# A recurrent attention block with a mixture of depths: weight loads on other turns, one product piece and one pair of PSUM banks exchanged

## The chip, the cores and the metric

The kernel runs on one core of a Trainium2 chip. The metric is the device time of one execution in microseconds, given as the median of several runs. Chunks, turns and batches are counted from 0.

## What is computed

For 4 batches, 8 heads and 768 time steps, with heads of 48, a recurrence carries a state matrix along the sequence:

```python
for t in range(S):
    cur = np.einsum('bhd,bhe->bhde', u[None] * kt, vt)
    y[:, :, t] = np.einsum('bhd,bhde->bhe', rt, state + cur)
    state = wt[:, :, :, None] * state + np.einsum('bhd,bhe->bhde', kt, vt)
```

The heads side by side make rows x of 384. In each batch the 128 rows with the highest score go through a two-layer network (384 to 1024 to 384), all others are left as they are:

```python
scores = np.einsum('bsd,d->bs', x, w_gate)
h = np.maximum(xe @ w1, 0.0)
ye = h @ w2
out[b, top_idx] = x[b, top_idx] + g[:, None] * ye   # g: sigmoid of the score
```

All data are float32.

## The kernel before

The sequence is cut into chunks of 128 steps: 6 to a batch, 24 in all (`N`). A chunk is computed with matrix products, and the state passes from chunk to chunk.

**The turn.** `turn(i)` (L661) writes out by hand the order in which instructions of several chunks are issued; each engine then works through its own list in that order. It runs for i from -2 to 24. Of what a turn holds, these steps matter here:

- `scores(i)` (L337) makes `ps_s`; `masked(i)` (L347) multiplies it on VectorE into `sc`.
- `compared(i - 2)` (L462) transposes the scores of a chunk's rows into `ps_e` (L478, TensorE), counts on VectorE which rows beat which (L480, L484), and keeps a copy by ScalarE (L489). In turn 23 there is a second one, for chunk 22, after `outputs_t(23)` (L695).
- `rows_out(i - 1)` (L390) transposes a chunk's results into `ps_y`, adds a part on GpSimd, or on VectorE in the last two turns (L401), and stores the rows (L408). In those two turns `row_scores_soon` (L425) makes the rows' scores on VectorE as well.
- `inputs_t` (L307) transposes r of chunk i + 1, and at the end of the turn k of chunk i + 2, into `ps_t`. `decays_t` (L245) does the same with the decays, and `scans` (L249) makes their running products on VectorE, both for chunk i + 2. `own_products` (L315, GpSimd) multiplies r and k of chunk i + 1.
- `outputs_t(i)` (L364) makes `ps_yt` from `sc`, v and the state; `carry_products(i)` (L445) makes `ps_kv`, though not for a batch's last chunk.
- `loads(i + 5)` (L140) issues four transfers of 192 KB from SyncE: v of chunk i + 3, k and r of chunk i + 4, w of chunk i + 5. k, r and w have four buffers each, v five.
- `load_weights(1)` (L711) issues, from turn 2 on, one of seven pieces of the two weight matrices in each turn, also from SyncE: three of w1 with 512 KB and then four of w2 with 384 KB.

SyncE issues all loads, weight pieces and stores in one order. Two more kinds of DMA, the gather of the picked rows and the scatter of their results, are issued by GpSimd.

**The mixture.** When a batch's last chunk has been compared, `mixture(b)` (L491) ranks its rows (`ps_r`, `rank`), finds the indices of the picked ones (`ps_i`, `idx`), gathers them (`xe`, L546) and transposes them (`ps_x`, then `xeT`, L557). `forward` (L578) then is a Python generator of pieces. Eight pieces of first-layer products (L590) come first, each of six matmuls into a quarter of a tile `ps_h`. The first four pieces fill one tile and the last four another, and after each tile ScalarE takes the ReLU into `hid` (L595). Eight pieces of second-layer products (L600) into `ps_f` follow. VectorE then makes `ye` (L607) from `ps_f`, and GpSimd scatters it (L610). `fed(n)` (L638) issues the next n pieces, and `fed_in_turn` (L653) does so twice in a turn. For batch 2 some pieces are kept for the end: of its first-layer pieces the fourth and fifth come in turn 23, the sixth and seventh in turn 24, and the last one after the loop, with the second layer.

**The banks.** All eight PSUM banks are taken. Tiles with the tag "m" share the one bank of `psM`, and tiles with the tag "y" that of `psY`. A tile's first matmul waits until the tile before it in that bank has been read. `ps_h` and `ps_f` are tiles of `psM`, `ps_y` of `psY`. `ended` is filled after the last turn (L719), when `ps_y` isn't needed any more; from then on a second tile of `ps_h` is made in `psY`. Batch 3, the last one, goes through `forward` wholly after that.

Of the kernel before, what the change touches and what calls it, by code (L numbers as in the profile page):

```python
# [38 lines left out]
def kernel(  # L39
# [47 lines left out]
    NCH = S // L  # L87
    HP = H // 2
    NDC = C // L
    NFC = F // L  # L90
# [13 lines left out]
    psY = ctx.enter_context(tc.tile_pool(name="psY", bufs=1, space=PSUM))  # L104
    psK = ctx.enter_context(tc.tile_pool(name="psK", bufs=1, space=PSUM))
    psM = ctx.enter_context(tc.tile_pool(name="psM", bufs=1, space=PSUM))

    chunks = [(b, ci) for b in range(B) for ci in range(NCH)]
    N = len(chunks)
# [30 lines left out]
    def loads(n):  # L140
        load(v_bufs, v, n - 2)
        load(k_bufs, k, n - 1)
        load(r_bufs, r, n - 1)
        load(w_bufs, w, n)
# [12 lines left out]
    for bufs, x, n in ((r_bufs, r, 1), (w_bufs, w, 2), (v_bufs, v, 0)):  # L157
# [8 lines left out]
    weights = [  # L166
        (w1[:, i, :], moe_w1[i * L:(i + 1) * L, :]) for i in range(NDC)
    ] + [
        (w2[:, i:i + 2, :], moe_w2[i * L:(i + 2) * L, :].rearrange("(n p) c -> p n c", p=L))
        for i in range(0, NFC, 2)  # L170
    ]

    def load_weights(n):
        while n > 0 and weights:
            to, src = weights.pop(0)
            nc.sync.dma_start(out=to, in_=src)
            n -= 1
# [54 lines left out]
    def warm(n):  # L232

        ps = psM.tile([L, 512], FP32, tag="m", name="ps_n")
        for _ in range(n):
            nc.tensor.matmul(ps, nothing[:, 0:L], nothing, start=True, stop=True)
# [39 lines left out]
    def check_sums():  # L276

        above = setup.tile([L, 1], FP32)
        nc.vector.tensor_reduce(out=above, in_=guard, axis=AX.X, op=ALU.add)
        below = setup.tile([L, 1], FP32)  # L280
        junk = setup.tile([L, N * HP], FP32)
        nc.vector.tensor_scalar(
            out=junk, in0=alls.rearrange("p n j -> p (n j)"), scalar1=float(LOW ** L),
            scalar2=None, op0=ALU.is_lt, op1=ALU.add, accum_out=below,
        )
        return above, below
# [291 lines left out]
    def forward(b, n, idx, xe, xeT, gate, gated):  # L578

        hid = mod.tile([L, NFC, L], FP32, name="hid")
        for f0 in range(0, NFC, 4):

            pool, tag = (psY, "y") if ended and f0 % 8 == 4 else (psM, "m")
            ps = pool.tile([L, 4, L], FP32, tag=tag, name="ps_h")
            for q in range(4):
                for dc in range(NDC):
                    nc.tensor.matmul(  # L590
                        ps[:, q, :], w1[:, dc, (f0 + q) * L:(f0 + q + 1) * L],
                        xeT[:, dc, :], start=(dc == 0), stop=(dc == NDC - 1),
                    )
                if q == 3:
                    nc.scalar.activation(out=hid[:, f0:f0 + 4, :], in_=ps, func=AF.Relu)  # L595
                yield q == 3

        ps = psM.tile([L, C], FP32, tag="m", name="ps_f")
        for fc in range(NFC):
            nc.tensor.matmul(  # L600
                ps, hid[:, fc, :], w2[:, fc, :], start=(fc == 0), stop=(fc == NFC - 1)
            )
            yield fc == NFC - 1
        while not gated:
            mix()
        ye = mod.tile([L, C], FP32, name="ye", bufs=2)
        nc.vector.scalar_tensor_tensor(  # L607
            out=ye, in0=ps, scalar=gate, in1=xe, op0=ALU.mult, op1=ALU.add
        )
        nc.gpsimd.indirect_dma_start(  # L610
            out=views[b][0:b + 1].rearrange("b s c -> (b s) c"),
            out_offset=bass.IndirectOffsetOnAxis(ap=idx[0:n, 0:1], axis=0),
            in_=ye[0:n], in_offset=None,
            bounds_check=(b + 1) * S - 1, oob_is_err=False,
        )
        yield True
# [3 lines left out]
    mixing, picked, feed, ended, sums = [], [], [], [], []  # L620

    def step(f, n, *more):
        if 0 <= n < N:
            f(work.setdefault(n, dict(n=n)), *more)

    def mix(n=1, place=None):


        while n > 0 and mixing:
            if place is not None and mixing[0][1] not in (None, place):  # L630
                return
            try:
                mixing[0][1] = next(mixing[0][0])
                n -= 1
            except StopIteration:
                mixing.pop(0)

    def fed(n, on=True):  # L638

        while n > 0:  # L640
            if not feed:
                if not picked:
                    return
                feed.append((picked[0][0], forward(*picked.pop(0))))
            try:
                last = next(feed[0][1])
                n -= 1
                if last and not on:
                    return
            except StopIteration:  # L650
                feed.pop(0)

    def fed_in_turn(n, few):  # L653

        kept = (feed or picked) and (feed or picked)[0][0] == B - 2
        fed(few if kept else n, on=False)

    PIECES = -(-2 * NFC * len(groups) // NCH)


    def turn(i):  # L661
        soon = i >= N - 1
        step(first_left, i + 1)
        step(own_products, i + 1)
        step(scores, i)
        step(own_values, i)
        step(carry, i - 1, work.get(i))
        step(scaled, i + 1, "K", "right")
        step(own_weights, i + 1)
        if soon:  # L670
            step(masked, i)
        if i == N - 1:
            sums.extend(check_sums())
        if i < N:
            step(compared, i - 2)
        if not soon:
            step(masked, i)
        step(back, i)
        if i == 0:
            warm(6)  # L680
        mix(place="half")
        step(rows_out, i - 1, soon)
        step(row_scores_soon if soon else row_products, i - 1)
        step(own_results, i)
        fed_in_turn(PIECES // 2, 2 if i >= N - 1 else 1)
        step(inputs_t, i + 1, "R", r_bufs)
        if i == -1:
            warm(4)
        step(scaled, i + 1, "R", "left")
        step(decays_t, i + 2)  # L690
        mix(place="mid")
        if i == -2:
            warm(2)
        step(range_check, i + 2)
        step(outputs_t, i)  # L695
        if i == N - 1:
            step(compared, i - 1)
        step(carry_products, i)
        fed_in_turn(PIECES - PIECES // 2, 1 if i == N - 1 else 0)
        step(inputs_t, i + 2, "K", k_bufs)  # L700
        if i == -2:
            warm(1)
        if not soon:
            step(row_sums, i - 1)
        step(scans, i + 2)
        if 0 <= i - 2 < N - 1 and chunks[i - 2][1] == NCH - 1:
            mixing.append([mixture(chunks[i - 2][0]), "end"])
        mix(place="end")
        if i > -2:
            loads(i + 5)  # L710
        if i > 1:  # L711
            load_weights(1 if NCH > 2 else 100)

    with tc.manual_schedule():
        warm(6)
        for i in range(-2, N + 1):
            turn(i)

        ended.append(True)  # L719
        mix(1000)  # L720
        mixing.append([mixture(B - 1), "half"])
        step(compared, N - 1)
        fed(1)
        mix()
        wide = checked(sums)
        fed(1)
        mix()
        fed(NFC - 2)
        mix(2)
        fed(2)  # L730
        mix(1000)
        fed(1000)
        outside = nc.values_load(wide, min_val=0, max_val=1)
# [72 lines left out]
```

## Time and profile before

| what | value |
|---|---|
| median of 3 runs | 207.44 us (207.41 to 207.98) |
| the profiled execution | 208.35 us |
| its span, first to last instruction | 206.6 us |
| mean granted TensorE clock | 0.994 |
| busy: PE / DVE / ACT / POOL | 193.0 / 161.4 / 123.4 / 133.2 us |
| DMA moved | 29.20 MB in 105,671 packets, 100,512 of them under 512 B |
| share of the hardware queue q1 | 71.4% of 16 engines' span |
| weight pieces, issue to landing | 5.9 us (512 KB), 5.0 us (384 KB) |
| loads of k, issue to landing | 5.2 us |

PE is TensorE's matmuls, PEld its weight loads, DVE VectorE, ACT ScalarE, POOL GpSimd, SP SyncE; SPq is SyncE issuing DMAs. Times in the views are microseconds from the span's start. In a list in order of time each line gives start, length, engine, line of the kernel and operation, then what is written and read; in square brackets stands how long the engine idled before it and what ended that. Matmuls are pipelined, so two neighbours overlap by a tenth or two. The row of DMA shares cuts the span into 40 slices of 5.2 us; a digit is the busy share of the DMA engines in tenths.

Turns can be told apart by their `ps_s`: that of turn 0 starts at 9.54 us, of turn 5 at 40.25, of turn 7 at 52.31, of turn 10 at 75.99, of turn 23 at 173.18. The first first-layer product of batch 0 starts at 73.95, its first second-layer product at 95.54.

### The profile page before, as it was taken

What the parts mean: (1) busy time and instruction counts of PE and PEld (TensorE: products, weight loads), DVE (VectorE), ACT (ScalarE), POOL (GpSimd) and SP (SyncE); (2) the same over time, 40 slices, a digit from 0 to 9 for tenths busy, and PEclk for the clock granted to TensorE, in tenths of its full rate; (3) what the DMA queues carried; (4) which work ended last, traced back from release to release, by engine and by line L of the source; (5) the groups of instructions that cost most, each with busy time, mean ns of one, the idle gap of its engine ahead of it and who ended that gap; (6) DMA issues with size and microseconds to landing.
All of it is one profiled execution on the core that took longest, in us unless ns stands there. A gap on an engine that the chain in (4) does not pass through costs nothing.

```text
span 206.6 us, 6425 instructions
## 1 busy us (share of the span) xinstructions
PE 193.0 (93%) x2302; PEld 157.1 (76%) x2303; DVE 161.4 (78%) x350; ACT 123.4 (60%) x642; POOL 133.2 (64%) x165
## 2 busy tenths in 40 slices
PE   7999999988889899999999999999999999898980
PEld 3668888767777788898887888897787898775940
DVE  5999999999979968988869888979868984851010
ACT  7177977768754765878355866787545776310300
POOL 6366899886847996668538898668638896122101
PEclk9999999999999999999999999999999999999997
DMA  6999999798988999998992994998553211111101
GB/s 113 186 163 177 167 179 203 187 168 233 248 188 182 241 237 193 202 193 180 208 155 77 154 203 99 132 179 150 121 86 90 56 49 41 38 43 40 38 8 43
DMA packets 105671, 29.20 MB, mean 141 GB/s; under 512 B 100512, under 2 KB 104864, under 8 KB 105632
## 3 DMA queue, kind: packets, MB, share of 16 engines
q1 hardware_dynamic: 105120, 27.14, 71.4%
q0 software_dynamic: 512, 1.57, 2.5%
q8 instruction: 20, 0.33, 0.7%
q14 instruction: 19, 0.16, 0.3%
HBM read 23.20 MB, written 5.51 MB: 139 GB/s over the span
## 4 chain that ended last, share of the span: by engine, by line
PE 77%; DMA 9%; SPq 4%; DVE 2%; POOL 2%; issue 2%; ACT 1%; POOLq 0%; DVEq 0%
PE ps_t L242 12%; PE ps_h L590 11%; PE ps_f L600 11%; PE ps_s L342 11%; PE ps_yt L375 10%; DMA k_buf<-in_k_dram 9%; PE ps_yt L383 5%; PE ps_y L242 5%; PE ps_w L242 4%; PE ps_kv L437 4%; SPq L135 3%; PE ps_e L478 3%; PE ps_r L504 1%; ACT rk L327 1%; PE ps_x L555 1%
## 5 line engine op out<-in xcount | busy, mean ns | idle before, releaser
L327 ACT ACTIVATE rk<-rk 128x48 f32<-128x48 f32 x192 | 43.6, 231 | 0.0
L327 ACT ACTIVATION_READ_ACCUMULATOR rk<-rk 128x1 f32 x192 | 36.3, 189 | 0.0
L407 POOL TENSOR_TENSOR x<-x,vo 128x384 f32<-128x384 f32 x22 | 22.1, 1005 | 21.0 <-ACT x L405 20.8
L266 DVE TENSOR_TENSOR_SCAN left<-ps_w,from_left 128x511 f32<-128x511 f32 x24 | 30.7, 1281 | 0.9
L388 ACT COPY yt<-ps_yt 128x512 f32<-128x512 f32 x24 | 14.0, 585 | 28.3 <-PE ps_yt L383 25.0
L255 DVE TENSOR_TENSOR_SCAN right_buf<-ps_w,from_right 128x511 f32<-128x511 f32 x24 | 29.1, 1212 | 1.7 <-PE ps_w L242 1.7
L318 POOL TENSOR_TENSOR rk<-r_buf,k_buf 128x384 f32<-128x384 f32 x24 | 24.2, 1007 | 9.1 <-DMA r_buf<-in_r_dram 9.1
L350 DVE TENSOR_TENSOR sc<-ps_s,before_f 128x1024 f32<-128x1024 f32 x24 | 29.3, 1220 | 0.8 <-PE ps_s L342 0.8
L342 PE MATMUL ps_s<-R,K 48*128 48x128 f32 x384 | 27.9, 285 | 0.3 <-ACT yt L388 0.2
L375 PE MATMUL ps_yt<-sc,v_buf 128*64 128x128 f32 x384 | 26.3, 278 | 1.4 <-PE ps_w L242 1.2
L342 PEld LDWEIGHTS ps_s<-R,K 48*128 48x128 f32 x384 | 23.3, 187 | 3.9 <-issue 2.5
L590 PE MATMUL ps_h<-xeT,w 128*128 128x128 f32 x192 | 25.3, 279 | 0.8 <-DVE ye L607 0.8
L321 POOL TENSOR_TENSOR rk<-rk,u_bc 128x384 f32<-128x384 f32 x24 | 24.1, 1004 | 2.4 <-DMA u_bc<-in_u_dram 1.8
L375 PEld LDWEIGHTS ps_yt<-sc,v_buf 128*64 128x64 f32 x384 | 20.6, 136 | 5.7 <-issue 2.7
L590 PEld LDWEIGHTS ps_h<-xeT,w 128*128 128x128 f32 x192 | 23.0, 192 | 2.0 <-ACT xeT L557 1.4
L600 PE MATMUL ps_f<-w,hid 128*128 128x384 f32 x64 | 23.8, 499 | 0.0
L412 POOL TENSOR_TENSOR scr<-x,wg_bc 128x384 f32<-128x384 f32 x22 | 22.0, 1002 | 1.7
L333 POOL TENSOR_TENSOR vo<-v_buf,own 128x384 f32<-128x384 f32 x24 | 20.0, 832 | 1.6 <-ACT rk L327 1.3
L313 DVE TENSOR_TENSOR K<-ps_t,right_buf 128x512 f32<-128x512 f32 x24 | 16.4, 683 | 4.9 <-PE ps_t L242 4.9
L313 DVE TENSOR_TENSOR R<-ps_t,left 128x512 f32<-128x512 f32 x24 | 16.5, 686 | 3.9 <-ACT own L569 1.6
L242 PE MATMUL ps_t<-ident,k_buf 128*128 128x128 f32 x96 | 15.2, 281 | 1.8 <-DMA k_buf<-in_k_dram 1.8
L242 PE MATMUL ps_w<-ident,w_buf 128*128 128x128 f32 x96 | 15.3, 284 | 0.7 <-ACT every L489 0.7
(102 smaller groups left out, 349.1 us busy)
## 6 DMA issues: line engine op xcount, KB each, us to landing
k_buf<-in_k_dram SPq DMA_DIRECT2D x24, 192.0 KB, 5.2
r_buf<-in_r_dram SPq DMA_DIRECT2D x24, 192.0 KB, 5.3
v_buf<-in_v_dram SPq DMA_DIRECT2D x24, 192.0 KB, 4.9
out_dram<-x SPq DMA_DIRECT2D x24, 192.0 KB, 3.1
w_buf<-in_w_dram SPq DMA_DIRECT2D x23, 192.0 KB, 4.8
w<-in_moe_w_dram SPq DMA_DIRECT2D x3, 512.0 KB, 5.9
w<-in_moe_w_dram SPq DMA_DIRECT2D x4, 384.0 KB, 5.0
w_buf<-in_w_dram SPq DMA_DIRECT2D x2, 96.0 KB, 2.4
```

The costliest lines, as they stand in the source:

```text
L242: nc.tensor.transpose(ps[:, j, :], src(j), ident)
L255: nc.vector.tensor_tensor_scan(out=flat[:, W - 2::-1], data0=wt[:, W - 1:0:-1], data1=from_right.rearrange("p j t -> p (j t)")[:, W - 2::- ...
L266: nc.vector.tensor_tensor_scan(out=left.rearrange("p j t -> p (j t)")[:, 1:W], data0=wt[:, 0:W - 1], data1=start.rearrange("p j t -> p (j ...
L313: nc.vector.tensor_mul(out, t.pop(name + "t"), t.pop(by))
L318: nc.gpsimd.tensor_mul(rk, r_bufs[n % NBUF][:, :, 0:D], k_bufs[n % NBUF][:, :, 0:D])
L321: nc.gpsimd.tensor_mul(t["rk"], t["rk"], u_bc)
L327: nc.scalar.activation(out=rk[:, h, :], in_=rk[:, h, :], func=AF.Copy, accum_out=o[:, h:h + 1])
L342: nc.tensor.matmul(ps[:, q, j, :], t["K"][rows, j, :], t["R"][rows, j, :], start=True, stop=True,)
L350: nc.vector.tensor_mul(t["sc"].rearrange("p q j t -> p (q j) t"), ps.rearrange("p q j t -> p (q j) t"), _heads(before_f, 2 * HP),)
L375: nc.tensor.matmul(ps[half(c), j % 2, j // 2, :], vt[:, 2 * j + q, :], t["sc"][:, q, j, :], start=(j < 2), stop=(old is None), skip_group_ ...
L590: nc.tensor.matmul(ps[:, q, :], w1[:, dc, (f0 + q) * L:(f0 + q + 1) * L], xeT[:, dc, :], start=(dc == 0), stop=(dc == NDC - 1),)
L600: nc.tensor.matmul(ps, hid[:, fc, :], w2[:, fc, :], start=(fc == 0), stop=(fc == NFC - 1))
```

## The change

```diff
+        load_weights(len(weights) - NFC // 2)
         hid = mod.tile([L, NFC, L], FP32, name="hid")
         for f0 in range(0, NFC, 4):
-            pool, tag = (psY, "y") if ended and f0 % 8 == 4 else (psM, "m")
+            pool, tag = (psY, "y") if ended and f0 % 8 == 0 else (psM, "m")
             ps = pool.tile([L, 4, L], FP32, tag=tag, name="ps_h")
...
+        load_weights(len(weights))
         ps = psM.tile([L, C], FP32, tag="m", name="ps_f")
...
+    WEIGHT_TURNS = list(range(2, 2 * NDC + 2, 2)) + list(range(2 * NDC + 1, 100))
...
         step(outputs_t, i)
+        step(carry_products, i)
+        fed_in_turn(PIECES - PIECES // 2, 1 if i == N - 1 else 0)
         if i == N - 1:
             step(compared, i - 1)
-        step(carry_products, i)
-        fed_in_turn(PIECES - PIECES // 2, 1 if i == N - 1 else 0)
         step(inputs_t, i + 2, "K", k_bufs)
...
-        if i > 1:
-            load_weights(1 if NCH > 2 else 100)
+        if i in WEIGHT_TURNS:
+            load_weights(1)
```

Three things differ. **The weights:** with `NDC` = 3 the seven pieces are issued at the ends of turns 2, 4, 6 (w1) and 7, 8, 9, 10 (w2), where before it was turns 2 to 8. The two calls inside `forward` load what is still missing when a forward pass begins and when its second layer begins; at these shapes nothing is missing there, so they issue nothing. **The piece:** in turn 23 the second group of forward work, one piece of batch 2's second tile of `ps_h`, is issued before `compared` of chunk 22 and no longer after it. `carry_products` has nothing to do in that turn, and in all other turns the order is as it was. **The banks:** once `ended` is filled, the first tile of `ps_h` lies in `psY` and the second in `psM`.

## Prediction

> **What bounds the kernel now.** I read the page's first two parts, then the chain that ended last, then the instructions in order of time around each of the three places that the change touches, and SyncE's own queue. On the page TensorE is busy 93% of the span, and the row of DMA shares stays at nine tenths until some two thirds of the way.
>
> ```profile
> span 206.6 us, 6425 instructions
> ...
> DMA  6999999798988999998992994998553211111101
> ```
>
> So two things are full at once: TensorE everywhere, and the DMA engines until about slice 27. From 10 to 46 us a turn of the chunk loop takes 5.8 to 6.1 us, TensorE and VectorE both being full (in the stretch 34 to 40 us PE is busy 5.86 and DVE 5.89 of 6.00); from 76 to 167.5 us PE is busy for the whole of every stretch that I asked for. Between them, and at the end, the chain leaves the engines:
>
> ```profile
> 45.04 6.58 DMA k_buf<-in_k_dram
> 51.76 0.64 PE ps_t L242 x4
> 52.93 6.09 DMA k_buf<-in_k_dram
> 59.16 0.63 PE ps_t L242 x4
> ```
>
> The columns are start, length, what. Twice the transposition of k (`inputs_t`, L307) waits for its transfer: for chunk 8 at 51.76, for chunk 9 at 59.16. The chain takes the second transfer for a follower of the first transposition; since no buffer of it is still in use then, I read it as the load queue's own backlog.
>
> **Why the transfers are late.** SyncE issues all loads and stores in one order. Its rows:
>
> ```profile
> 31.62 0.66 SPq L135 DMA_DIRECT2D k_buf<-in_k_dram  x1
> ...
> 36.38 0.84 SPq L176 DMA_DIRECT2D w<-in_moe_w_dram  x1
> ...
> 38.27 0.85 SPq L135 DMA_DIRECT2D k_buf<-in_k_dram  x1
> ...
> 45.04 2.39 SPq L135 DMA_DIRECT2D k_buf<-in_k_dram  x1
> ...
> 52.93 0.48 SPq L135 DMA_DIRECT2D k_buf<-in_k_dram  x1
> ```
>
> These are k of chunks 6, 7, 8 and 9 (the loads that end turns 2 to 5). Before them k was issued at 21.06 and 26.22: 5.16 and 5.40 us apart, no weight piece between. With one 512 KB piece of w1 between (36.38, 43.32, 50.78) the distances are 6.65, 6.77 and 7.89. A piece thus costs the queue 7.10 - 5.28 = 1.8 us by the means, 1.25 (6.65 - 5.40) to 2.7 (7.89 - 5.16) by the ends. A turn is only 6 us long, so the queue falls back each time until the lead of two turns is used up.
>
> **Part 1, the weights.** Seven SyncE issues stay seven, with the same bytes. Until now they close turns 2 to 8; then they close 2, 4, 6 (w1) and 7 to 10 (w2). In front of k of chunk 9 there are two pieces in place of three, so it is issued about 1.8 us earlier and lands at 52.93 + 6.09 - 1.8 = 57.2. It is wanted when the products before it end:
>
> ```profile
> 57.83 0.67 PE L437 MATMUL ps_kv<-v_buf,kt 128*64 128x48 f32 x16
> ...
> 58.30 1.28 DVE L266 TENSOR_TENSOR_SCAN left<-ps_w,from_left 128x511 f32<-128x511 f32 x1
> ...
> 59.16 0.63 PE L242 MATMUL ps_t<-ident,k_buf 128*128 128x128 f32 x4 [0.65 <-DMA k_buf<-in_k_dram]
> ...
> 60.56 0.18 DVE L514 TENSOR_REDUCE rank<-ps_r 128x6 f32<-128x18 f32 x1 [0.99 <-PE ps_r L509]
> ```
>
> That is 58.51, so the wait of 0.65 goes even at the low price of 1.25 (57.8). Is anything late next? VectorE ends its scan at 59.58 and then idles 0.99 until TensorE has made the ranks, so it takes the 0.65 up in full. GpSimd waits 1.87 for r of chunk 9 until 60.13; r follows k in the queue and comes earlier with it. Everything after hangs on those two engines, and from 76 us TensorE is full, so the 0.65 stays: **-0.65**.
>
> The wait for chunk 8 (0.49 at 51.76) goes as well, but I give it nothing: VectorE runs from scan to scan without a gap there and multiplies k of chunk 8 only at 53.23, and `ps_yt` at 56.23 waits for that row of work. So the part lies between 0 and 0.65 + 0.49 = 1.14.
>
> The Trainium skill, "DMA: Bandwidth & Descriptors", Specifications, speaks against a large effect: it puts line rate at transfers of 512 B and more, and about 358 GB/s for one core's HBM, so that pieces with long rows would be the cheap ones and the loads with rows of 192 B the dear ones. An estimate from that page makes a 512 KB piece 1.46 us, and the 0.65 would still go; the measured spacing stands here.
>
> What the later pieces could cost: the third of w1 now closes turn 6. The old place there ended with an issue at 65.44 (landing 5.9, so 71.3 with both other pieces still in front), and the first first-layer product starts at 73.95, or 73.3 once it is shifted: cover 2.0 us, and some 3 more since two pieces fewer stand in front. Each microsecond beyond costs one. The four of w2 close turns whose w loads end at 71.5, 78.3, 85.6 and 90.5; landing 5.0 makes 76.5 to 95.5, against uses at 95.5, 99.7, 104 and 112. Nothing waits. At each point of the queue no more pieces have gone than before, so k and r of chunks 10 to 15 don't get later.
>
> **Part 2, the piece in front of the scores.** In turn 23 one piece (six matmuls, no other engine) changes places with `compared` of chunk 22 (one PE instruction, L478; its DVE and ACT instructions keep their order):
>
> ```profile
> 176.87 0.60 ACT L595 ACTIVATE hid<-ps_h 128x512 f32<-128x512 f32 x1
> ...
> 177.95 0.29 PE L478 MATMUL ps_e<-ident,score 128*128 128x128 f32 x1 [0.60 <-DVE score L425]
> ...
> 178.09 0.83 PE L590 MATMUL ps_h<-xeT,w 128*128 128x128 f32 x6
> ...
> 178.75 0.60 PE L242 MATMUL ps_y<-ident,yt 128*128 128x128 f32 x4
> ...
> 179.45 0.62 DVE L401 TENSOR_TENSOR x<-ps_y,vo 128x192 f32<-128x192 f32 x2 [0.49 <-issue]
> ```
>
> TensorE idles 0.60 for the score. The piece needs psM, which the ReLU on ACT frees at 177.47. A waiting matmul starts 0.05 us after an ACT copy (`yt` ends 173.13, `ps_s` at 173.18) to 0.14 after DVE (`ye` ends 189.69, next 189.83). So: piece 177.52 to 177.61, ps_e 0.66 later, ps_y 0.14 after that, 178.32 to 178.41 against 178.75. Queued behind the new wait are ps_e and ps_y; ps_e would then end near 178.5, and DVE wants it at 178.60, so a tenth is left. DVE waits for ps_y (0.49 idle), and from there the scores, ranks, gather and last forward pass follow in one line. **-0.38**, between 0 (ReLU as late as the score) and 0.60.
>
> **Part 3, the banks.** Only the last batch's forward pass comes under `ended` when its tiles are made (both tiles of batch 2 are made in or before turn 23). Its first 24 products move from psM to psY, its second 24 from psY to psM. Before, the first wait 0.80 at 189.83 for `ye` to empty psM:
>
> ```profile
> 189.07 0.62 DVE L607 SCALAR_TENSOR_TENSOR ye<-ps_f,gate,xe 128x384 f32<-128x384 f32 x1 [4.73 <-PE ps_f L600]
> ...
> 189.83 5.60 PE L590 MATMUL ps_h<-xeT,w 128*128 128x128 f32 x48 [0.80 <-DVE ye L607]
> ...
> 195.26 5.33 PE L600 MATMUL ps_f<-w,hid 128*128 128x384 f32 x16
> ...
> 195.46 0.60 ACT L595 ACTIVATE hid<-ps_h 128x512 f32<-128x512 f32 x1 [2.06 <-PE ps_h L590]
> ```
>
> After, they need only xeT, ready at 188.42 + 0.48 = 188.90. With a hand-over of x they start at 188.90 + x and end 5.60 later. But `ps_f` is made in psM too, now the bank of the second half, and must wait for that half's ReLU: 0.03 + 0.60 + x more, so 195.13 + 2x against 195.26. With x from 0.05 to 0.14 that is -0.03 to +0.15. The old order hid this ReLU behind ps_f's first eight matmuls. I take **+0.06**; unknown ends -0.80 (no repayment) and +0.9 (no refund).
>
> **Sum.** -0.65 - 0.38 + 0.06 = -0.97 on the profiled execution of 208.35 (span 206.6 and 1.75 around it): 207.38. The median shown is 207.44, 0.91 below the profiled one; the same difference gives 206.47, say 206.5.
>
> **Rivals.** *Forecast*, 0.62: 205.85 to 206.75 by its ends (tail part 0.34 to 0.43, weights 0.5 to 1.14). *VectorE takes the wait's place*, 0.20: if the 0.65 is swallowed as the 0.49 is, -0.32 is left: 207.1. For it: DVE 5.89 of 6.00; against it: the 0.99 before the ranks. *The piece taken out frees too little*, 0.07: the change then doesn't do what it says, k of chunk 9 stays late because the backlog was there before the weights (the issues already lag the turns); it needs less than 0.65 freed, under half of the smallest distance measured. Again 207.1. *The bank swap isn't repaid*, 0.05: 205.7. *Slower*, 0.06: the third w1 piece comes after its user at 73.3. Price one for one; it turns the sign when the landing is past 73.3 + 0.97 = 74.3, so an issue after 68.4, 3 us later than the old place; at 75.5 the time would be 208.7.
>
> A measurement tells about 0.3% (0.62 us) from no change. Faster: 0.62 + 0.05 = 0.67; within: 0.20 + 0.07 = 0.27; slower 0.06. The range 205.8 to 207.3 takes in the forecast and the two cases at 207.1 and leaves out the last two, with some of the edges.
>
> **What would show it.** Right: no wait for k near 59, chunk 9's issue near 51, DVE's idle time before `rank` down to some 0.3; the ps_h of six ahead of ps_e with no 0.60 wait; ps_h of 48 starting right after xeT, and a new wait of ps_f for ACT's ReLU of 0.6 to 0.9. Wrong: `ps_yt` or `rank` coming at the same distance from 46 us as before, the first ps_h waiting for a weight, or ps_f not waiting.

## The result, and the profile after

| | median | executions |
|---|---|---|
| before | 207.43 us | 207.30, 207.41, 207.44, 207.98 |
| changed | 207.44 us | 207.28, 207.35, 207.54, 207.67 |

The ratio is 0.9996 with a 95% interval of 0.9975 to 1.0017: no change that this comparison can tell, where 206.5 us was forecast. In the ratios and counts below, executions more than 1.5% over the fastest of their kernel are left out (three in all). Yet the two profiles look as the forecast had it. The changed kernel's profiled execution took 207.28 us (span 205.5), the one of before 208.35 (span 206.6). So the profiles are 1.07 us apart, 0.97 was forecast, and the medians don't move. That is the question of what follows.

First the lines that answer to those shown of before. From the list in order of time of the changed kernel, around the transposition of k of chunk 9:

```profile
57.75 0.67 PE L437 MATMUL ps_kv<-v_buf,kt 128*64 128x48 f32 x16
...
58.21 1.28 DVE L266 TENSOR_TENSOR_SCAN left<-ps_w,from_left 128x511 f32<-128x511 f32 x1
...
58.35 0.66 PE L242 MATMUL ps_t<-ident,k_buf 128*128 128x128 f32 x4
...
59.79 0.18 DVE L514 TENSOR_REDUCE rank<-ps_r 128x6 f32<-128x18 f32 x1 [0.30 <-PE ps_r L509]
```

The wait of 0.65 for k is gone, and VectorE's idle time before `rank` fell from 0.99 to 0.30, as forecast. SyncE's rows of the same kernel (k of chunks 8 and 9, and the second w1 piece between them):

```profile
43.84 0.91 SPq L135 DMA_DIRECT2D k_buf<-in_k_dram  x1
...
48.05 0.89 SPq L176 DMA_DIRECT2D w<-in_moe_w_dram  x1
...
50.40 0.48 SPq L135 DMA_DIRECT2D k_buf<-in_k_dram  x1
```

k of chunk 9 is issued at 50.40, where the profile of before had 52.93. Next turn 23, the piece that now stands in front of the scores' transposition:

```profile
175.96 0.60 ACT L596 ACTIVATE hid<-ps_h 128x512 f32<-128x512 f32 x1
...
176.61 0.94 PE L591 MATMUL ps_h<-xeT,w 128*128 128x128 f32 x6 [0.18 <-ACT hid L596]
...
177.38 0.27 PE L478 MATMUL ps_e<-ident,score 128*128 128x128 f32 x1
...
177.49 0.60 PE L242 MATMUL ps_y<-ident,yt 128*128 128x128 f32 x4
...
178.19 0.62 DVE L401 TENSOR_TENSOR x<-ps_y,vo 128x192 f32<-128x192 f32 x2
```

The scores of turn 23 start at 172.27 here and at 173.18 before. From there to ps_y it is 5.22 us in place of 5.57: 0.35 won, 0.38 forecast. The piece waits 0.18 for the ReLU, ps_e no longer waits for its score, and VectorE no longer idles 0.49 before L401. Last the final forward pass:

```profile
187.69 5.62 PE L591 MATMUL ps_h<-xeT,w 128*128 128x128 f32 x48
...
187.80 0.62 DVE L609 SCALAR_TENSOR_TENSOR ye<-ps_f,gate,xe 128x384 f32<-128x384 f32 x1 [4.73 <-PE ps_f L602]
...
193.35 0.60 ACT L596 ACTIVATE hid<-ps_h 128x512 f32<-128x512 f32 x1 [1.21 <-PE ps_h L591]
...
194.00 5.43 PE L602 MATMUL ps_f<-w,hid 128*128 128x384 f32 x16 [0.69 <-ACT hid L596]
```

The first-layer products start 0.11 us before `ye` does, where they used to start 0.76 after it (0.87 won). And there is the new wait: ps_f 0.69 for the ReLU. From the start of ps_h to that of ps_f it is 6.31 where it was 5.43 (0.88 lost). From one `ye` to the next it is 11.66 against 11.56.

### The profile page after: what moved, and what is told of

Same layout as the page of the kernel before. It is cut to its first block, busy times and chain, and to the rows that moved or that the text cites. A ratio compares the mean times of both kernels' runs of the same rounds, so it can differ in the third digit from the quotient of the medians.

```text
span 205.5 us, 6424 instructions
## 1 busy us (share of the span) xinstructions
PE 192.5 (94%) x2303; PEld 156.7 (76%) x2303; DVE 161.2 (78%) x350; ACT 123.4 (60%) x642; POOL 133.2 (65%) x165
## 4 chain that ended last, share of the span: by engine, by line
PE 81%; SPq 4%; DVE 4%; DMA 3%; ACT 2%; POOL 2%; issue 2%; POOLq 0%; DVEq 0%; ACTq 0%
PE ps_t L242 12%; PE ps_s L342 11%; PE ps_h L591 11%; PE ps_f L602 11%; PE ps_yt L375 10%; PE ps_yt L383 5%; PE ps_y L242 5%; PE ps_w L242 5%; PE ps_kv L437 5%; SPq L135 3%; PE ps_e L478 3%; DMA k_buf<-in_k_dram 3%; PE ps_r L504 1%; ACT rk L327 1%; PE ps_x L555 1%
## 5 line engine op out<-in xcount | busy, mean ns | idle before, releaser
L302 ACT ACTIVATE junk<-w_buf,high 128x384 f32<-128x384 f32 x24 | 15.1, 630 | 1.6 <-DMA w_buf<-in_w_dram 1.6
```

## The experiments

Two theories. **A**: the waits for k belong to the execution that was profiled and not to the median. That execution took 208.35 us where the others took 207.3 to 207.98. The transfers then are just in time in most executions and late in some, and moving the weights saves only in the latter. **B**: the waits are in every execution, and the moved weights cost as much elsewhere. Each kernel ran on the same chip as the kernel before, whose median there is given beside it.

### The kernel before, once more

No edit. 

> The kernel before, unchanged, profiled once more. Theory A (the waits for k at 51.76 and 59.16 belong to that one execution, which took 208.35 us where most take 207.4): the scores of turn 10 start near 75.0 us and no longer at 75.9, k of chunk 9 makes TensorE wait under 0.2 us, and the span is near 205.7. Theory B (the waits are in every execution of the kernel before, and the changed weights cost as much elsewhere): turn 10 starts at 75.9 again, span 206.5. Time ratio 1.000 by both.

Measured: 207.76 us (207.46 to 208.49, 12 executions) beside 207.93 (207.51 to 209.74) of the same kernel, ratio 0.9989 (0.9974 to 1.0005). Its profiled execution took 207.53 us, span 205.8. The same stretch, order of time (one line of SyncE first):

```profile
51.61 0.44 SPq L135 DMA_DIRECT2D k_buf<-in_k_dram  x1
...
57.86 0.67 PE L437 MATMUL ps_kv<-v_buf,kt 128*64 128x48 f32 x16
...
58.47 0.65 PE L242 MATMUL ps_t<-ident,k_buf 128*128 128x128 f32 x4
...
59.27 1.00 POOL L318 TENSOR_TENSOR rk<-r_buf,k_buf 128x384 f32<-128x384 f32 x1 [0.97 <-DMA r_buf<-in_r_dram]
...
59.90 0.18 DVE L514 TENSOR_REDUCE rank<-ps_r 128x6 f32<-128x18 f32 x1 [0.29 <-PE ps_r L509]
```

The unchanged kernel has no wait for k here: the scores of turn 10 start at 75.11 where the same list of the first profile has 75.92 (75.99 in the chain), and `rank` idles 0.29, as in the changed kernel. k of chunk 9 was issued 1.3 us sooner (51.61 for 52.93) with the weights on the same turns, so the queue's own speed differs that much from one execution to the next. B falls, since this execution has no wait; A stands.

One more thing is read here. In the first profile k of chunk 8 was 0.49 us late, here it isn't, and ps_kv of turn 7 starts at 57.83 there and 57.86 here. So that wait did cost nothing, as the prediction had it.

### The weights alone

```diff
-        if i > 1:
-            load_weights(1 if NCH > 2 else 100)
+        if i in WEIGHT_TURNS:
+            load_weights(1)
```

> Only the weight pieces are moved (turns 2, 4, 6, 7 to 10). Theory A: the same time as before within 0.1 per cent, turn 10 near 75.0 us. Theory B: 0.1 to 0.3 per cent slower, with new idle time of TensorE between 60 and 110 us. The prediction's own step, if it held in the median: 0.65 us, 0.3 per cent, faster.

Measured: 207.64 us (207.37 to 208.15) beside 207.93, ratio 0.998 (0.9966 to 0.9994); turn 10 at 75.21 us. That is more than A's 0.1%, and far from B. The gain shows in the upper executions. The fastest are 207.37 here and 207.46 in the previous experiment; the slowest 208.15 here, while of the 35 executions of before beside it twelve took over 208.2.

### The piece alone

```diff
+        step(carry_products, i)
+        fed_in_turn(PIECES - PIECES // 2, 1 if i == N - 1 else 0)
         if i == N - 1:
             step(compared, i - 1)
-        step(carry_products, i)
-        fed_in_turn(PIECES - PIECES // 2, 1 if i == N - 1 else 0)
```

> Only the piece is put in front of the second comparison in turn 23. Both theories: 0.36 us faster (ratio 0.998), the distance from the scores of turn 23 to the ye of batch 2 falls from 15.89 to 15.53 us. If the tail's saving isn't real: 1.000.

Measured: ratio 0.9984 (0.996 to 1.0008), so by time alone inconclusive. Inside the tail of its profile it is 5.23 us from the scores of turn 23 to ps_y (5.57 before) and 15.54 to the `ye` of batch 2 (15.89). The saving of 0.34 to 0.35 is the piece's.

The profiled execution itself took 210.52 us (span 208.8). Up to turn 10 this kernel does the same as the one before, with the weights on their old turns, and there its excess lies: the transpositions of k of chunks 8 and 9 wait again, and longer.

```profile
52.29 0.63 PE L242 MATMUL ps_t<-ident,k_buf 128*128 128x128 f32 x4 [0.71 <-DMA k_buf<-in_k_dram]
...
60.46 1.02 PE L242 MATMUL ps_t<-ident,k_buf 128*128 128x128 f32 x4 [1.65 <-DMA k_buf<-in_k_dram]
```

From the scores of turn 10 to those of turn 23 it is 97.27 us, against 97.26 in the repeated kernel before. So this is a second long execution that shows the wait for k. The wait for chunk 8 again cost nothing: ps_kv of turn 7 starts 17.66 us after the scores of turn 5, as in the first profile of before (17.65 in the repeated one). From turn 5 to turn 10 it took 2.98 us more than the repeated kernel, with a wait of 1.65 for chunk 9; the granted clock was low just after that wait, which the last section shows.

### The banks alone

```diff
-            pool, tag = (psY, "y") if ended and f0 % 8 == 4 else (psM, "m")
+            pool, tag = (psY, "y") if ended and f0 % 8 == 0 else (psM, "m")
```

> Only the banks of the last forward pass are exchanged. Both theories: 0.05 to 0.15 us slower (ratio 1.0005), the distance from the ye of batch 2 to the ye of batch 3 grows from 11.56 to 11.66 us: the wait of 0.8 in front of the first products is gone and one of about 0.7 stands in front of ps_f. If the new wait is dearer than the profile shows: 1.002 and more.

Measured: 208.03 us (207.78 to 209.42) beside 207.93, ratio 1.0013 (0.9994 to 1.0032): not told from no change. By the profile it is 11.66 us from one `ye` to the next, 0.10 more than before, with the same wait of 0.69 before ps_f as in the changed kernel. The exchange of banks moves a wait from one place to the other.

### Two pieces per turn

```diff
-            load_weights(1 if NCH > 2 else 100)
+            load_weights(2)
```

> Two weight pieces per turn from turn 2 on (turns 2, 3, 4, and one in 5) in place of one per turn: the suspected backlog doubled, nothing else changed. Theory A (the queue of loads has about a microsecond in hand in most executions, and waits when the weights or a slow spell use it up): k of chunks 7, 8 and 9 is issued 1.8 to 4 us later and now waits in every execution; the fastest execution is at least 1 us above the fastest of before, the median 2 to 5 us above. Rival (transfers are late by chance only, and the weights have no part in it): the same time as before, within 0.2 per cent.

Measured: 210.67 us (210.49 to 211.24) beside 207.91, ratio 1.0123 (1.0095 to 1.0151), and the fastest execution 3.0 us above the fastest of before. The transpositions of k of chunks 8 and 9:

```profile
53.08 0.63 PE L242 MATMUL ps_t<-ident,k_buf 128*128 128x128 f32 x4 [1.49 <-DMA k_buf<-in_k_dram]
...
60.88 0.63 PE L242 MATMUL ps_t<-ident,k_buf 128*128 128x128 f32 x4 [1.85 <-DMA k_buf<-in_k_dram]
```

The weights in front of k do make it late. The rival, chance alone, falls. k of chunk 9 was issued at 54.61 here, with six pieces in front of it in place of three: 1.5 to 3.7 us later than in the five profiles with three (50.90 to 53.09).

### The changed kernel, twice more

No edit. 

> The changed kernel once more, with more executions. Theory A: its fastest executions lie 0.2 to 0.3 us under the fastest of before (tail: -0.35 for the piece, +0.10 for the banks), nearly none has the wait for k, so the median is 0.3 to 0.6 us under that of before (ratio 0.9975 to 0.9985). If the change is worth nothing: 1.000.

> The changed kernel a third time, to see whether the ratio of 0.997 of the second series or the 0.9996 of the first holds. Theory A (a third of the executions of before carry the wait, almost none of the changed kernel, and 0.26 us of the tail in all): 0.9960 to 0.9985, and a median below that of before by 0.3 to 0.6 us. If the second series was chance: 0.999 to 1.001.

Measured: 207.47 us (207.02 to 208.09) beside 207.91, ratio 0.9969 (0.9951 to 0.9987); and 207.26 (206.95 to 208.06) beside 207.84, ratio 0.997 (0.9955 to 0.9985), with 12 executions of the changed kernel each time. Both series say 0.3% faster. The first comparison's interval (0.9975 to 1.0017) overlaps both; it had four executions a side, and its four of before lay low, by chance as far as is known: median 207.43, where its three series beside the other kernels have 207.84 to 207.93. The fastest executions of the changed kernel lie 0.47 and 0.51 us under the fastest of before, where 0.2 to 0.3 was expected; which step gives the other 0.2 isn't shown.

### The changed kernel with ps_f in psY

```diff
+        late = bool(ended)
         hid = mod.tile([L, NFC, L], FP32, name="hid")
...
-        ps = psM.tile([L, C], FP32, tag="m", name="ps_f")
+        pool, tag = (psY, "y") if late else (psM, "m")
+        ps = pool.tile([L, C], FP32, tag=tag, name="ps_f")
```

> The changed kernel, but the last ps_f is made in psY too, which the ReLU of the first half empties about 2 us before it is needed; so the first products don't wait, and neither does ps_f. Theory: the wait of 0.69 before ps_f goes, ye of batch 3 comes 0.8 to 0.9 us earlier after ye of batch 2 (10.8 for 11.66), and the time is 0.85 us under the changed kernel, about 1.2 us under before (ratio 0.994). Rival (ps_f must wait for the second half's ReLU in any case, because it reads hid): no change against the changed kernel.

Measured: 206.46 us (206.29 to 206.70) beside 207.91, ratio 0.9922 (0.9898 to 0.9945). This beats both kernels. Its last second layer, in order of time:

```profile
193.32 5.33 PE L604 MATMUL ps_f<-w,hid 128*128 128x384 f32 x16
...
193.52 0.60 ACT L597 ACTIVATE hid<-ps_h 128x512 f32<-128x512 f32 x1 [1.22 <-PE ps_h L592]
```

ps_f starts before the second half's ReLU; 10.71 us lie between one `ye` and the next, 0.95 less than with ps_f in psM. The early start of ps_h, which the change had handed back, is now kept.

### The same tail with the weights on their old turns

The piece's and the banks' edits and the edit above; the weights as before. 

> The piece, the exchanged banks and ps_f in psY, with the weights on their old turns. Theory A: fastest executions as with the weights moved (e7), but a third of the executions 0.7 to 1.1 us longer, median 0.1 to 0.4 us above e7. If the weights' turns don't matter: equal to e7 in median and in spread.

Measured: 207.00 us (206.16 to 207.79) beside 207.91, ratio 0.9955 (0.9936 to 0.9974). The fastest execution is that of the kernel above (206.16 for 206.29), the median is 0.54 higher (0.1 to 0.4 was expected), and the spread is 1.6 us in place of 0.4. The moved weights take away the upper executions and leave the fastest where it was.

### No piece in front of k of chunk 9

```diff
-    WEIGHT_TURNS = list(range(2, 2 * NDC + 2, 2)) + list(range(2 * NDC + 1, 100))
+    WEIGHT_TURNS = list(range(5, 100))
```

> The kernel of e7, but the weight pieces close turns 5 to 11, so that none stands in front of k of chunk 9. Theory A (the moved weights already take the wait out of nearly every execution): k of chunk 9 is issued before 50 us, and median and spread are those of e7 within 0.1 per cent (206.3 to 206.7). If two pieces in front still cost something: 0.2 us or more under e7. If the third piece of w1 is now late for the first product of batch 0 (near 73 us): slower by what it is late.

Measured: 206.41 us (206.23 to 206.66) beside 207.84, ratio 0.9931 (0.9915 to 0.9947): equal to the kernel with two pieces in front. k of chunk 9 was issued at 47.5, 2.9 us sooner than in the changed kernel, and nothing came of it. Two pieces in front already leave it in time, and the third w1 piece, now issued at 66.0, isn't late either (turn 10 starts at 75.12).

## Why the prediction was wrong

**The failed step** is the last line of the sum: "The median shown is 207.44, 0.91 below the profiled one; the same difference gives 206.47". It takes the 0.65 off a median that mostly doesn't hold it. The wait for k of chunk 9 is most of what made the profiled execution longer than the median. The profiles show it place by place. Turn 5 to turn 10 is the distance between their scores in the lists in order of time:

| profiled execution | k of chunk 9 issued | TensorE waits for it | turn 5 to turn 10 |
|---|---|---|---|
| before, 208.35 us | 52.93 | 0.65 | 35.75 |
| before once more, 207.53 | 51.61 | none | 34.90 |
| the piece alone, 210.52 | 53.09 | 1.65 | 37.88 |
| the banks alone, 207.83 | 51.94 | none | 34.90 |
| ps_f in psY, old turns, 206.45 | 50.90 | none | 34.90 |
| two pieces per turn, 211.24 | 54.61 | 1.85 | 38.49 |
| the six with weights moved | 47.46 to 50.68 | none | 34.90 to 34.91 |

Without the wait the stretch takes the same 34.90 us whichever turns the weights have; in these profiles it is longer where k of chunk 9 is late, and nowhere else. Of the five profiles with one piece a turn on the old turns two have the wait, of the six with the weights moved none. The times of unprofiled executions fit. Of the 87 executions of before in the later series, 24 took 0.74 us or more over the fastest (207.46). All four kernels with the old turns together have 39 of 122 executions that far over their own fastest, the five series with the weights moved 3 of 48. That these executions are long for the same reason is likely, but only a profile shows the wait itself. So the 0.65 is saved in about a third of executions, and the median moves by part of it: 0.29 us between the weights alone and before. With the 0.26 of the tail that makes 0.55; the two long series of the changed kernel measured 0.44 and 0.58, not 0.97.

The other steps, one by one:

- **What bounds the kernel**: right. The load queue's backlog makes k late, and the weights make the backlog (210.67 us with two pieces a turn).
- **1.8 us for a piece**: of the right size, but not a constant. With three pieces in front k of chunk 9 was issued at 50.90 to 53.09 (mean 52.09, five profiles), with two at 50.20 to 50.68 (mean 50.35, five profiles): 1.7 us by the means. None in front makes it another 2.9 earlier for two pieces, six make it 2.5 later than the mean for three. With three in front the issue also differs more between executions, by 2.2 us against 0.5 with two. The price was enough either way, since an issue at 51.94 still brought no wait and one at 52.93 did.
- **-0.65 for k of chunk 9**: right between the two profiles, if small. From turn 6 to turn 10 it is 29.87 us before and 29.03 after, 0.84. Of the 0.19 that I had missed, 0.15 is the picks, told below. In the median it is the mis-sized term.
- **Nothing for k of chunk 8**: right, by the repeated profile of before.
- **No loss from the later pieces**: right. The third w1 piece is issued at 60.24 in the changed kernel, the last of w2 near 88, and no product waits for either.
- **-0.38 for the piece**: 0.34 to 0.36. **+0.06 for the banks**: 0.10, though not by the hand-over: ps_f starts 6.19 us after `ye` starts before and 6.20 after, and what grows is its own length, 5.33 to 5.43. The tail as a whole, from the scores of turn 23 to the last `ye`, takes 27.45 us before and 27.19 in the changed kernel, 0.26 less.
- **The range** (205.8 to 207.3) ended under 207.44 because it was built around the profiled execution. The rival at 207.1 came nearest, but its reason, VectorE swallowing the wait, wasn't seen: `rank` took the 0.65 up in full.

What stays open is why, with the old turns, the queue issues k of chunk 9 up to 2.2 us sooner or later from one execution to the next. Nothing here varied it on purpose, except by the weights.

## What to carry to other kernels

A profile is one execution: when it is longer than the median by about as much as the wait that is to be removed, that wait may be what made it long, and the gain must not be taken off the median. A second profile of the same kernel helps to tell. Transfers that arrive just in time spread the times rather than shift them, so a change to them is judged by spread and by enough executions (a dozen a side here, where four told nothing). When a tile gets another bank, ask which tile comes after it in that bank: here the early start came back as a wait of the same size, and a third placement kept it.

## What the runs showed of the hardware

**A VectorE operation beside GpSimd.** VectorE's first of six `pick` operations was longer in the profile of before than in the others. First the operation's lengths there (the columns: count, then least, median and greatest length in ns, first and last start), then in the repeated kernel before:

```profile
L524 DVE TENSOR_SCALAR pick<-slots,rank x6: 243/243/410, 60.8 to 61.8; 128x128 bf16<-128x128 bf16 x6
```

```profile
L524 DVE TENSOR_SCALAR pick<-slots,rank x6: 248/248/257, 60.1 to 60.9; 128x128 bf16<-128x128 bf16 x6
```

In the first the pick starts at 60.77 while GpSimd multiplies from 60.13 to 61.13, and it ends at 61.18, 0.05 after GpSimd does. In the second GpSimd's multiplication ends at 60.27, some 0.16 after the first pick starts, and the pick has its usual length (257). So a late r, by way of a late GpSimd multiplication, cost VectorE another 0.15. The profile with two pieces per turn has the case once more, and smaller: GpSimd multiplies until 62.73, the first pick starts at 62.50 and takes 280 ns, so it too ends 0.05 after GpSimd does. In the other ten profiles no pick takes more than 257. The Trainium skill, "SBUF — State Buffer", Who interferes with whom, states that a VectorE operation of this kind can take a pair of ports that it shares with GpSimd, and that the second to issue blocks until the first has finished. The rows agree with that; no experiment here was made for it.

**The granted clock after a long wait.** Two profiles have a wait of more than 1.6 us for k of chunk 9, and in both TensorE's granted clock falls just after it. The rows of the clock (40 slices, tenths of full speed, 9 being 90% or more), for the piece alone and for two pieces per turn:

```profile
PEclk9999999999975999999999999999999999999998
```

```profile
PEclk9999999999995999999999999999999999999999
```

From 60 to 68 us the first has a mean clock of 0.57, from 62 to 70 the second; the 16 products of `ps_s` that start there take 2.08 us in both, where 1.16 is usual. The wait of 0.65 in the profile of before brought nothing of the kind (1.00 from 48 to 74). So in these two executions the late transfer cost more than the wait that the list shows. Where between 0.65 and 1.65 us this begins, and whether the wait alone brings it, no run here shows.
